# One pool of four PSUM banks, value copies for batch 0, and new costs in a planned attention and mixing kernel

## The chip, the cores and the metric

The kernel runs on one core of a Trainium2 chip. The metric is the device time of one execution in microseconds (us), as the median of several runs. The core's engines are TensorE (PE in the profile, with PEld for its weight loads), VectorE (DVE), ScalarE (ACT), GpSimd (POOL) and SyncE (SP); SP issues all DMA transfers here. TensorE writes its results into PSUM, which has eight banks of 512 fp32 words per partition.

## The reference, cut to what matters

Sizes: 8 batches, 8 heads of 64, 512 local and 32 global positions (544 rows), model width 512, hidden width 2048.

```python
# attention: a global part over all 544 keys, and a local part over a band of 65 keys and the 32 global ones
out_g = softmax(scale * q_g @ k_all.T) @ v_all
out_l = softmax([scale * q_l @ k_g.T, where(|i - j| <= 32, scale * q_l @ k_l.T, -1e9)]) @ [v_g, v_l]
x = concat(out_g, out_l) as (8, 544, 512)
# mixing and a feed-forward net
u = x + real(fft(fft(x, axis=1), axis=2))
un = (u - mean(u)) / sqrt(var(u) + 1e-6)
y = u + relu(un @ w_ch1) @ w_ch2
```

## The kernel before, in words

**Stages.** The heads of a batch are taken in four pairs p (32 pairs in all, four per batch). A pair has four units u of 128 queries. For two units together `scores` (L576) makes 24 small matmuls into the two banks of one tile S, one bank per head; `masked` (L590) on DVE adds the mask and takes the row maximum, `exps`, `p_hi` (ACT) and `p_lo` (POOL) turn that into fp16 high and low parts, `turn` (SP) transposes them by DMA into pl, and `values` (L622) multiplies with the values into a bank, from which `norm` (DVE) makes x. Two pairs form a group g, for which `g_scores`, `g_max`, `g_exp`, `g_turn`, `g_values` and `g_norm` do the same for the global queries. `x_out` stores a pair's x in DRAM. Once a batch's pairs are done, `jobs_dft` loads x back and makes the two Fourier transforms as matmuls (`d_first` L885, `d_second` L925), which gives u. The 4352 rows make 17 chunks of 256, two per batch and a last one of the 32 rows that each batch leaves over: `l_bn` to `l_turn` normalise a chunk, `f_first` (L1030) makes the hidden layer in eight steps of 24 matmuls, `f_hi` and `f_lo` evict it, and `f_second` (L1050) makes eight steps of 12 matmuls into two accumulator banks.

**Weights.** Both weight matrices come as 32 tiles of 64-bit floats. `w_load` (SP) fetches a tile into a buffer, `w_split64` (ACT) and `w_low` (POOL or ACT) take its halves, `w_size` (DVE) joins them, `w_sum` (L383, PE) sums absolute values, `w_sign` (DVE) sets the signs, `w_max` finds a scale for a group of tiles, and `w_hi` (ACT) and `w_lo` (DVE, L428) make the fp16 parts. The first `f_first` waits for the last `w_sum` (the object `wend`).

**The plan.** The order of all instructions on every engine is made on the host. `Plan.add` declares a job: engine, a cost in us, what it reads and writes, a due time t, a margin. `Plan.run` plays the jobs through with these costs: on each engine the job with the earliest due time goes next among those that are ready, and the order that results is written out (`emit`); on the chip each engine runs its list in that order, and semaphores do the waiting. A margin delays the moment from which a job counts as ready after its inputs. `rate` multiplies the declared cost of TensorE's attention jobs (`PEF` = 1.65 for pairs 0 to 3). The due times of the units of batch 0 come from `U_AT` and `U_PACE`: U_AT + U_PACE·k for unit k. Those of the weight tiles come from `W_AT`, `W2_AT` and others, and those of the chunks from `T0` and `PERIOD`. `QUEUE` limits how far ahead of the DMA work a load of q, k, v or weights is issued.

**PSUM.** The eight banks are: S (two banks, one buffer, shared by `scores` and `g_scores`), two for `ps1` (hidden layer, and weights), two accumulators (`acc0`, `acc1`), and `bk` and `bk1`, a pool of two for the outputs of `values` and of the Fourier transforms. In `bk` there are also fixed columns that the pool does not know: the result of `g_values` (columns 300 to 364) and small totals (`total` L420, `dft_scale` L764, columns from 400 on).

**Batch 0 and its values.** A unit's keys lie in two row blocks, and the second block is 96 rows: 64 local ones and 32 global ones, which lie apart in vN. For batches 1 to 7 `v_out` (L545) copies them together into vB with two DMAs per pair, and `values` makes 12 matmuls per unit (per head three of 128 rows and three of 96). For batch 0 there is no copy, and in three of a pair's four units each matmul of 96 rows is made as one of 64 and one of 32 rows.

Of the kernel before, what the change touches and what calls it, by code (L numbers as in the profile page):

```python
# [33 lines left out]
U_AT, U_PACE = 16.0, 2.0  # L34
# [8 lines left out]
PEM, SPM = 0.6, 0.2  # L43
LOOK = {"ACT": 0.5, "DVE": 0.5, "POOL": 0.8, "SP": 0.5}
ALOW = 4
L_HOLD = 50.0
QUEUE = 2.0
# [55 lines left out]
class Plan:  # L103
# [64 lines left out]
    def run(self):  # L168
# [20 lines left out]
        def ready(j):  # L189
# [5 lines left out]
            for d in j.war:  # L195
                t = max(t, d.end if d.eng == j.eng and not d.svc else d.end + self.HOP)
            for o in j.alloc:
                k = o[0]
                if k in self.pools:
                    v = [0.0 if h is None else done_at[h] if left[h] == 0 else None for h in pool[k]]  # L200
                    v = [x for x in v if x is not None]
                    if not v:
                        return None
                    t = max(t, min(v) + self.HOP)
                else:
                    h = hold[k][count[k] % len(hold[k])]
                    if h is not None:
                        if left[h]:
                            return None
                        t = max(t, done_at[h] + self.HOP)  # L210
# [6 lines left out]
        while todo:  # L217
# [28 lines left out]
            for o in j.alloc:  # L246
                k = o[0]
                if k in self.pools:
                    for i, h in enumerate(pool[k]):
                        if h is None or (left[h] == 0 and done_at[h] <= s + 1e-9):  # L250
                            pool[k][i] = o
                            self.slot[o] = i
                            break
# [20 lines left out]
class Kern:  # L274
    def __init__(self, tc, stack, ins, out):
# [49 lines left out]
        self.bk, self.bk1 = (self.ps.tile([P, 512], F32, name=f"bk{i}") for i in range(2))  # L325
# [92 lines left out]
    def total(self, a, n):  # L418
        o = 400 + 8 * n if n < 8 else 400 + 4 * n
        w = math.prod(a.shape[1:])  # L420
        pb = self.bk[:, o:o + w]
# [73 lines left out]
    def z_total(self, g):  # L495
        self.total(self.acc[g % 2], g % 8)
# [7 lines left out]
    def scales(self, g):  # L504
# [5 lines left out]
        self.scale_of(z[:, :, 3:6], g % 8)  # L510
# [64 lines left out]
    def scores(self, i):  # L575
# [3 lines left out]
        js = (2 * half, 2 * half + 1)  # L579
        s["S"] = S = self.psa.tile([P, 2, 512], F32, name="S", tag="A", bufs=1)  # L580
        for n, j in enumerate(js):
            for o in range(2):
                for m, (a, c) in enumerate(((0, 0), (0, 1), (1, 0))):
                    k0 = 512 * c + P * j
                    for h in range(2):
                        r = slice(64 * h, 64 * h + 64)
                        t = 224 * n
                        ps, k = (S[:, h, t + 192:t + 224], kg[r, c]) if o else (S[:, h, t:t + 192], kT[r, k0:k0 + 192])
                        nc.tensor.matmul(ps, qT[r, a, j], k, start=m == 0, stop=m == 2)  # L589

    def masked(self, u):
# [3 lines left out]
        S, z = s["S"], s["z"]  # L595
        for h in range(2):
            nc.vector.tensor_tensor_reduce(self.per[u % 4][:, h, 0:224], S[:, h, 224 * n:224 * n + 224], self.msk[:, j], z[:, 8:9], 3e38,  # L597
# [21 lines left out]
    def bank(self, o):  # L619
        return (self.bk, self.bk1)[self.plan.slot[o]]  # L620

    def values(self, i):  # L622
# [31 lines left out]
    def g_scores(self, g):  # L654
        nc, G = self.nc, self.G[g]
        G["sg"] = S = self.psa.tile([P, 2, 512], F32, name="S", tag="A", bufs=1)
        for m, (a, c) in enumerate(((0, 0), (0, 1), (1, 0))):
            for o in range(2):
                for i in range(2):
# [3 lines left out]
                    nc.tensor.matmul(S[64 * i:64 * i + 64, o, 0:k.shape[1]], qg, k, start=m == 0, stop=m == 2)  # L663

    def g_max(self, g):
        nc, G = self.nc, self.G[g]
        G["ng"] = ng = self.p2.tile([P, 3], F32, name="ng")
        nc.vector.tensor_reduce(ng[:, 0:1], G["sg"][:, 0], axis=EX, op=ALU.max)
        nc.vector.tensor_reduce(ng[:, 1:2], G["sg"][:, 1, 0:SG], axis=EX, op=ALU.max)
        nc.vector.tensor_scalar(ng[:, 2:3], ng[:, 0:1], ng[:, 1:2], G["z"][:, 2:3], op0=ALU.max, op1=ALU.mult)  # L670

    def g_exp(self, g):
        nc, G, pg = self.nc, self.G[g], self.pg
        sg, ng, c = G.pop("sg"), G.pop("ng"), G["z"][:, 1:2]
        nc.scalar.activation(pg[:, 32:544], sg[:, 0], AF.Exp, bias=ng[:, 2:3], scale=c)
        nc.scalar.activation(pg[:, 576:608], sg[:, 1, 0:SG], AF.Exp, bias=ng[:, 2:3], scale=c)
# [87 lines left out]
    def dft_scale(self, b):  # L764
        nc = self.nc
        pb = self.bk[:, 496 + 8 * (b % 2):501 + 8 * (b % 2)]
# [372 lines left out]
    def jobs_scores(self, add, p):  # L1139
# [16 lines left out]
        if b:  # L1156
            add("SP", 1.16, self.v_out, p, r=[vN], w=[vB], svc=1.2, t=U[0] + 7)
# [220 lines left out]
```

## Time and profile before

| | us |
|---|---|
| median of 3 runs | 1067.12 (1066.3 to 1068.29) |
| the profiled execution | 1066.91 |
| its span, first to last instruction | 1064.8 |
| TensorE busy in it | 961.5 (90%) |
| VectorE busy | 709.1 (67%) |
| ScalarE busy | 583.4 (55%) |
| GpSimd busy | 442.7 (42%) |

The span is the profiled execution without 2.1 us around it. Busy time is the union of an engine's instructions. The row DMA is the mean busy share of 16 DMA engines. A wait is idle time of an engine just before an instruction, with the instruction elsewhere that ended it. A line such as L589 is the line of the kernel before.

### The profile page before, as it was taken

To read this page: it belongs to the slowest core of one execution; us is meant where nothing else is said; L and a number is where in the kernel's file an instruction comes from. 1 tells how busy PE (TensorE), PEld (TensorE's weight loads), DVE (VectorE), ACT (ScalarE), POOL (GpSimd) and SP (SyncE) were. 2 spreads that over 40 slices of the span, in tenths; PEclk is the share of its full clock that TensorE was granted. 3 is DMA by queue.
4 is the path that set the end of the run, shared out by engine and by line. 5 is a ranking of instruction groups with operands and counts; after the bars stand their busy time and mean duration, and the time that the engine had idled before them with its cause. 6 is when DMAs were issued, how large, how long until landed. Compare 5 with 4: busy or idle time off the path is not lost.

```text
span 1064.8 us, 25495 instructions
## 1 busy us (share of the span) xinstructions
PE 961.5 (90%) x9952; PEld 671.6 (63%) x9952; DVE 709.1 (67%) x1896; ACT 583.4 (55%) x1275; POOL 442.7 (42%) x604
## 2 busy tenths in 40 slices
PE   2598358989999999999999999899999999999996
PEld 1355136656676766676777777676766666666663
DVE  6877999977888677988767897897464232431111
ACT  7976786877666766876576768754131111111110
POOL 6765546754474465566257555744010110110000
PEclk9999978989999999999999999999999999999999
DMA  9989837956785866777668757875401102111000
GB/s 365 240 197 207 283 74 144 181 149 145 140 177 128 166 144 177 147 163 182 117 139 159 195 123 160 147 145 95 115 12 54 41 20 63 23 41 40 1 21 20
DMA packets 257889, 136.81 MB, mean 128 GB/s; under 512 B 201344, under 2 KB 235744, under 8 KB 257768
## 3 DMA queue, kind: packets, MB, share of 16 engines
q1 hardware_dynamic: 257768, 135.18, 55.1%
q8 instruction: 78, 1.28, 0.5%
q14 instruction: 43, 0.35, 0.1%
HBM read 64.88 MB, written 18.35 MB: 78 GB/s over the span
## 4 chain that ended last, share of the span: by engine, by line
PE 60%; DVE 14%; issue 2%; POOL 2%; ACT 1%; DMA 1%; SPq 0%; DVEq 0%; POOLq 0%; ACTq 0%
PE ps L1039 26%; PE acc L1058 25%; PE S L589 2%; PE bk L904 1%; PE bk L934 1%; PE bk L633 1%; DVE h L1048 1%; DVE pe L597 1%; PE bk L641 1%; DMA qk<-in_qk 1%; DVE wh L428 1%; PE S L663 1%; DVE x L824 1%; POOL ph L612 1%; DVE u L959 1%
## 5 line engine op out<-in xcount | busy, mean ns | idle before, releaser
L1039 PE MATMUL ps<-uh,wh 128*128 128x256 f16 x3264 | 380.2, 274 | 0.1
L1058 PE MATMUL acc<-wh,h 128*128 128x512 f16 x1632 | 374.5, 380 | 0.0
L1039 PEld LDWEIGHTS <-wh 128*128 128x128 f16 x3264 | 317.0, 98 | 53.3 <-issue 0.8
L1058 PEld LDWEIGHTS <-h 128*128 128x128 f16 x1632 | 156.0, 98 | 168.2 <-issue 2.8
L1048 DVE SCALAR_TENSOR_TENSOR h<-ps,h 128x512 f16<-128x512 f32 x136 | 93.7, 689 | 227.8 <-ACT h L1044 227.7
L1044 ACT ACTIVATE h<-ps 128x512 f16<-128x512 f32 x136 | 80.8, 594 | 278.5 <-PE ps L1039 278.2
L612 POOL TENSOR_TENSOR ph<-pe,ph 128x448 f16<-128x448 f32 x128 | 137.4, 1086 | 171.1 <-ACT ph L608 118.2
L604 ACT ACTIVATE pe<-pe,nm 128x224 f32<-128x224 f32 x256 | 103.9, 468 | 26.1 <-DVE nm L597 26.1
L597 DVE CUSTOM_DVE_ANT_0 pe<-S,msk,z 128x224 f32<-128x224 f32 x256 | 100.8, 445 | 7.1 <-PE S L589 5.4
L1019 POOL TENSOR_TENSOR ve<-ve 128x2 f32<-128x2 f32 x17 | 4.8, 285 | 204.6 <-DVE un L999 204.6
L633 PE MATMUL bk<-vN,pl 128*128 128x65 f16 x768 | 74.2, 200 | 12.4 <-DVE xg L709 3.8
L641 PEld LDWEIGHTS <-pl 96*128 96x128 f16 (+1 forms) x840 | 63.8, 100 | 23.0 <-issue 11.1
L608 ACT ACTIVATE ph<-pe 128x448 f16<-128x448 f32 x128 | 69.1, 564 | 8.1 <-DMA pl<-ph 6.8
L589 PE MATMUL S<-kT,qT 64*128 64x192 f16 x768 | 53.7, 263 | 21.0 <-DVE nm L597 16.9
L589 PEld LDWEIGHTS <-qT 64*128 64x128 f16 x1536 | 51.0, 99 | 30.7 <-DVE nm L597 17.3
L633 PEld LDWEIGHTS <-pl 128*128 128x128 f16 x768 | 59.0, 101 | 14.0 <-issue 3.8
L543 POOL TENSOR_TENSOR vN<-vf,vN 128x640 f16<-128x640 f32 x32 | 45.2, 1412 | 16.4 <-ACT vN L539 16.3
L532 POOL TENSOR_TENSOR vf<-vf,z 128x640 f32<-128x640 f32 x32 | 41.3, 1291 | 25.5 <-DVE z L499 24.5
L1003 ACT ACTIVATE unh<-un 128x512 f16<-128x512 f32 x34 | 21.3, 628 | 47.5 <-DVE un L999 47.3
L641 PE MATMUL bk<-vN,pl 96*128 96x65 f16 (+1 forms) x336 | 46.2, 214 | 0.0
L490 ACT ACTIVATE junk<-qk 128x512 f16<-128x512 f32 x64 | 39.8, 622 | 7.7 <-DMA qk<-in_qk 6.9
L552 ACT ACTIVATE qk<-qk,z 128x512 f32<-128x512 f32 x64 | 43.2, 708 | 0.0
(179 smaller groups left out, 1398.5 us busy)
## 6 DMA issues: line engine op xcount, KB each, us to landing
qk<-in_qk SPq DMA_DIRECT2D x32, 512.0 KB
vf<-in_v SPq DMA_DIRECT2D x32, 320.0 KB
xs<-x SPq DMA_DIRECT2D x32, 256.0 KB
out<-u SPq DMA_DIRECT2D x16, 512.0 KB
rx<-in_moe_w_ch SPq DMA_DIRECT2D x14, 512.0 KB
raw<-in_moe_w_ch SPq DMA_DIRECT2D x13, 512.0 KB
x<-xs SPq DMA_DIRECT2D x48, 128.0 KB
u<-xs SPq DMA_DIRECT2D x24, 256.0 KB
```

The source lines that it names most:

```text
L543: self.nc.gpsimd.tensor_sub(vN[:, :, 1, :, 0:64], self.st[p]["vf"], vN[:, :, 0, :, 0:64])
L589: nc.tensor.matmul(ps, qT[r, a, j], k, start=m == 0, stop=m == 2)
L597: nc.vector.tensor_tensor_reduce(self.per[u % 4][:, h, 0:224], S[:, h, 224 * n:224 * n + 224], self.msk[:, j], z[:, 8:9], 3e38, op0=ALU.ad ...
L604: self.nc.scalar.activation(pe[:, h, 0:224], pe[:, h, 0:224], AF.Exp, bias=nm[:, h:h + 1], scale=-1.0)
L608: self.nc.scalar.activation(ph[:, 0, :, 0:224], self.per[i % 4][:, :, 0:224], AF.Copy)
L612: self.nc.gpsimd.tensor_sub(ph[:, 1, :, 0:224], self.per[i % 4][:, :, 0:224], ph[:, 0, :, 0:224])
L633: nc.tensor.matmul(pv[:, j % 2, h], pl[:, 4 * a + 2 * h], vN[:, j, c, h, :], start=m == 0, stop=False)
L641: nc.tensor.matmul(pv[:, j % 2, h], pl[r:e, 4 * a + 2 * h + 1], v[:, c, h, :], start=False, stop=m == 2 and e == 96)
L1039: nc.tensor.matmul(ps[:, q], wt[:, w, c0:c0 + P], uh[:, :, 4 * a + kt, :], start=n == 0, stop=n == 11)
L1044: self.nc.scalar.activation(h[:, 0], self.fps[c, fp], AF.Relu)
L1048: self.nc.vector.scalar_tensor_tensor(h[:, 1], self.fps.pop((c, fp)), 0.0, h[:, 0], op0=ALU.max, op1=ALU.subtract)
L1058: nc.tensor.matmul(self.acc_f[c][j], h[:, a, q, j * P:(j + 1) * P], self.w[1, f][:, w, :], start=f == 0 and a == 0 and w == 0, stop=f == 1 ...
```

## The change

- The tile S goes, and `bk` becomes a list of four banks, one pool of four. `scores` takes two of them (one for each head), `g_scores` two, a pair of `values` one, `g_values` one (a job of the pool now, `pvg`), and each output of the Fourier transforms one, as before. The first bank of `g_scores` is never bank 0. A job that needs n banks waits until n are free, and takes those that have been free longest. The totals stay at fixed columns of bank 0 (from 448 on), with four places for the groups' totals in the place of eight, which the plan now counts (`zt`, `dt`).
- `v_out` runs for batch 0 too, and the split into 64 and 32 rows goes.
- The margin of TensorE's attention and Fourier jobs is 1.5 us in the place of 0.6, except for pairs 0 to 5 and the transforms of batch 0. It now counts after releases of buffers too, not only after inputs. `rate` 1.65 reaches to pair 5 (`EARLY`).
- `U_AT`, `U_PACE` go from 16, 2 to 4, 4, and `QUEUE` from 2 to 4.
- Declared costs of some twenty jobs change; no instruction of theirs does.

```diff
-U_AT, U_PACE = 16.0, 2.0
+U_AT, U_PACE = 4.0, 4.0
-PEM, SPM = 0.6, 0.2
+PEM, PEM0, SPM = 1.5, 0.6, 0.2
+EARLY = 6
-QUEUE = 2.0
+QUEUE = 4.0
...
             for d in j.war:
-                t = max(t, d.end if d.eng == j.eng and not d.svc else d.end + self.HOP)
+                t = max(t, d.end if d.eng == j.eng and not d.svc else d.end + self.HOP + j.margin)
...
-                    v = [x for x in v if x is not None]
-                    if not v:
+                    v = sorted(x for x in v if x is not None)
+                    n = sum(x[0] == k for x in j.alloc)
+                    if len(v) < n:
                         return None
-                    t = max(t, min(v) + self.HOP)
+                    t = max(t, v[n - 1] + self.HOP + j.margin)
...
-        self.bk, self.bk1 = (self.ps.tile([P, 512], F32, name=f"bk{i}") for i in range(2))
+        self.bk = [self.ps.tile([P, 512], F32, name=f"bk{i}") for i in range(4)]
...
-        s["S"] = S = self.psa.tile([P, 2, 512], F32, name="S", tag="A", bufs=1)
+        s["S", half] = S = [self.bank(("bank", "S", i, h)) for h in range(2)]
...
-                if j == 3:
-                    rest = [(0, 96, vN[0:96, 4])]
-                elif b:
-                    rest = [(0, 96, vB[:, j])]
-                else:
-                    rest = [(0, 64, vN[0:64, j + 1]), (64, 96, vN[64:96, 4])]
-                for r, e, v in rest:
-                    nc.tensor.matmul(pv[:, j % 2, h], pl[r:e, 4 * a + 2 * h + 1], v[:, c, h, :], start=False, stop=m == 2 and e == 96)
+                vb = vB[:, j, c, h, :] if j < 3 else vN[0:96, 4, c, h, :]
+                nc.tensor.matmul(pv[:, j % 2, h], pl[0:96, 4 * a + 2 * h + 1], vb, start=False, stop=m == 2)
...
-        G["pv"] = pv = self.bk[:, 300:365]
+        G["pv"] = pv = self.bank(("bank", "pvg", g))[:, 0:65]
...
-        if b:
-            add("SP", 1.16, self.v_out, p, r=[vN], w=[vB], svc=1.2, t=U[0] + 7)
+        add("SP", 1.16, self.v_out, p, r=[vN], w=[vB], svc=1.2, t=U[0] + 7)
...
-        rate = PEF if p < 4 else 1.0
+        rate, pem = (PEF, PEM0) if p < EARLY else (1.0, PEM)
...
-            add("DVE", .80, self.w_lo, k, i, r=[w], w=[h], t=T + 1)
+            add("DVE", 1.15, self.w_lo, k, i, r=[w], w=[h], t=T + 1)
...
-                add("DVE", 1.80, self.d_even, b, i, r=[x4h[0]], w=[x4h[0]], k=[x4])
+                add("DVE", 2.40, self.d_even, b, i, r=[x4h[0]], w=[x4h[0]], k=[x4])
...
-        plan = self.plan = Plan(rings, {"bank": 2})
+        plan = self.plan = Plan(rings, {"bank": 4})
```

## Rows read from the trace of the kernel before

**Rows 1.** Busy time by stretch: its us, then busy us (instructions) per engine.
```profile
core 0: us, PE busy (x) PEld busy (x) DVE busy (x) ACT busy (x) POOL busy (x), PEclk, DMA share, GB/s
0.00:42.00 42.00, 11.61 (x98) 6.88 (x98) 31.25 (x79) 34.53 (x75) 29.24 (x44) 1.00 0.92 319
42.00:108.00 66.00, 57.98 (x561) 36.70 (x562) 51.52 (x140) 48.66 (x105) 38.90 (x39) 1.00 0.90 214
108.00:161.00 53.00, 22.34 (x237) 15.46 (x235) 49.41 (x135) 41.82 (x95) 28.14 (x42) 0.86 0.59 170
161.00:250.00 89.00, 79.58 (x932) 56.70 (x930) 78.95 (x191) 64.92 (x145) 53.69 (x60) 0.93 0.77 160
250.00:750.00 500.00, 484.59 (x5971) 349.73 (x5972) 400.34 (x1154) 345.88 (x776) 277.52 (x362) 1.00 0.71 149
750.00:1065.00 315.00, 305.37 (x2160) 206.09 (x2158) 97.61 (x201) 47.59 (x84) 15.22 (x60) 0.99 0.13 36
```

**Rows 2.** TensorE in order of time: start, us, what; values of two units, batch 0.
```profile
55.07 0.24 PE L633 MATMUL bk<-vN,pl 128*128 128x65 f16 x1
55.24 0.40 PE L641 MATMUL bk<-vN,pl 64*128 64x65 f16 x2
...
58.04 0.23 PE L633 MATMUL bk<-vN,pl 128*128 128x65 f16 x1
58.09 0.25 PE L641 MATMUL bk<-vN,pl 96*128 96x65 f16 x1
...
58.81 0.66 PE L589 MATMUL S<-kT,qT 64*128 64x192 f16 x6
```

**Rows 3.** Waits of DVE and of SP from 42 to 108 us: total, times, longest.
```profile
DVE wm L395 <- PE wl L391: 7.9, 5, 2.6
DVE dng L707 <- PE bk L641: 3.0, 1, 3.0
...
SPq L617 <- PE bk L641: 5.0, 4, 3.6
```

**Rows 4.** SP and TensorE in order of time: the way to the first scores.
```profile
9.59 0.33 SPq L481 DMA_DIRECT2D vf<-in_v  x1
...
16.82 0.59 PE L423 MATMUL bk<-vac,part 128*128 128x6 f32 x2 [1.39 <-ACT junk L490]
...
23.25 0.34 PE L589 MATMUL S<-kT,qT 64*128 64x192 f16 x2 [0.92 <-ACT qT L562]
```

**Rows 5.** SP and TensorE in order of time: batch 0's last store to the first hidden layer.
```profile
109.22 0.38 SPq L732 DMA_DIRECT2D xs<-x  x1
...
122.65 0.53 SPq L547 DMA_DIRECT2D vB<-vN  x1
123.51 0.74 SPq L548 DMA_DIRECT2D vB<-vN  x1
...
160.82 6.32 PE L1039 MATMUL ps<-uh,wh 128*128 128x256 f16 x48
```

**Rows 6.** TensorE in order of time: scores after a wait, and two steps of f_first.
```profile
218.42 0.66 PE L589 MATMUL S<-kT,qT 64*128 64x192 f16 x6 [4.32 <-DVE nm L597]
...
220.10 4.75 PE L1039 MATMUL ps<-uh,wh 128*128 128x256 f16 x24
...
231.06 2.78 PE L1039 MATMUL ps<-uh,wh 128*128 128x256 f16 x24
```

**Rows 7.** Waits of TensorE from 250 to 750 us: total, times, longest.
```profile
PE bk L934 <- DVE xg L709: 2.9, 2, 1.5
PE S L589 <- DVE nm L597: 2.8, 3, 1.2
PE bk L633 <- DVE xg L709: 2.0, 2, 1.3
PE bk L633 <- DVE asm L951: 1.7, 2, 1.0
...
PE S L663 <- DVE nm L597: 1.1, 1, 1.1
PE bk L633 <- DVE z L924: 1.1, 1, 1.1
...
PE bk L423 <- DVE asm L951: 0.5, 1, 0.5
```

More of the change, by code (lines that the diff above doesn't have):

```diff
@@ L248, in run @@
                 if k in self.pools:
[L249 to L253, printed above, removed]
+                    n = len(pool[k])
+                    i = min((x for x in range(o[1:2] + o[3:] == ("Sg", 0), n) if pool[k][x] is None or left[pool[k][x]] == 0),
+                            key=lambda x: (-1.0 if pool[k][x] is None else done_at[pool[k][x]], x))
+                    pool[k][i] = o
+                    self.slot[o] = i
                 else:
@@ L578, in scores @@
         qT, kT, kg = s["qT"], s["kT"], s["kg"]
-        js = (2 * half, 2 * half + 1)
-        s["S"] = S = self.psa.tile([P, 2, 512], F32, name="S", tag="A", bufs=1)
-        for n, j in enumerate(js):
+        s["S", half] = S = [self.bank(("bank", "S", i, h)) for h in range(2)]
+        for n in range(2):
+            j = 2 * half + n
+            t = 224 * n
             for o in range(2):
@@ L655, in g_scores @@
         nc, G = self.nc, self.G[g]
-        G["sg"] = S = self.psa.tile([P, 2, 512], F32, name="S", tag="A", bufs=1)
+        G["sg"] = S = [self.bank(("bank", "Sg", g, o)) for o in range(2)]
         for m, (a, c) in enumerate(((0, 0), (0, 1), (1, 0))):
@@ L1155, in jobs_scores @@
         add("POOL", 1.35, self.v_lo, p, r=[vf, vN], w=[vN], t=U[0] + 5)
-        if b:
-            add("SP", 1.16, self.v_out, p, r=[vN], w=[vB], svc=1.2, t=U[0] + 7)
+        add("SP", 1.16, self.v_out, p, r=[vN], w=[vB], svc=1.2, t=U[0] + 7)
         x = ("x", p)
         def half(h):
-            i = 2 * p + h
-            S = ("S", i)
-            add("PE", rate * .76, self.scores, i, r=[kT, qT, kg], w=[S], t=U[2 * h], margin=PEM)
+            S = [("bank", "S", 2 * p + h, o) for o in range(2)]
+            add("PE", rate * .76, self.scores, 2 * p + h, r=[kT, qT, kg], w=S, t=U[2 * h], margin=pem)
             for n in range(2):
@@ L1166, in half @@
                 pe, ph = ("pe", u), ("ph", u)
-                add("DVE", .77, self.masked, u, r=[S, z, ("msk",)], w=[pe, ("nm", u)])
+                add("DVE", .77, self.masked, u, r=[*S, z, ("msk",)], w=[pe, ("nm", u)])
                 add("ACT", .77, self.exps, u, r=[pe, ("nm", u)], w=[pe])
@@ L1177, in vals @@
                 u = 4 * p + 2 * h + n
-                add("PE", rate * .42, self.values, u, r=[("pl", u), vN] + ([vB] if b else []), w=[pv], margin=PEM)
+                add("PE", rate * .42, self.values, u, r=[("pl", u), vN, vB], w=[pv], margin=pem)
             add("DVE", .80, self.norm, i, r=[pv, z], w=[x])
@@ L1230, in jobs_dft @@
             add("ACT", .63, self.d_hi, b, i, r=[*src, dsc], w=[eh[i]], k=own)
-            add("DVE", .90, self.d_lo, b, i, r=[*src, dsc, eh[i]], w=[eh[i]], k=own)
+            add("DVE", .70, self.d_lo, b, i, r=[*src, dsc, eh[i]], w=[eh[i]], k=own)
         add("ACT", 1.48, self.d_tail_hi, b, r=[et, dsc], w=[ht])
@@ L1248, in jobs_dft @@
                 pb = self.bank_of(b, (kt, cs))
-                add("PE", rate * .54, self.d_second, b, kt, cs, r=[(f"z{cs}", b), ("const",)] + ([("zr", b)] if cs == 0 else []), w=[pb], margin=PEM, **late)
+                add("PE", rate * .54, self.d_second, b, kt, cs, r=[(f"z{cs}", b), ("const",)] + ([("zr", b)] if cs == 0 else []), w=[pb], margin=pem, **late)
                 if cs == 0:
@@ L1256, in jobs_dft @@
             for i in range(2):
-                add("DVE", 1.00, self.d_add, b, kt, i, r=[asm] + ro + o[i:i + 1], w=o[i:i + 1], **late)
+                add("DVE", 1.25, self.d_add, b, kt, i, r=[asm] + ro + o[i:i + 1], w=o[i:i + 1], **late)
         add("SP", 1.3, self.d_rest, b, r=[("xf", b), ("xm", b)], w=[("ul", b)], svc=.3)
@@ L1274, in jobs_chunk @@
             un, hl = ("un", c, j), ("unh", c, j)
-            add("DVE", .50, self.l_un, c, j, r=rj + [ve], w=[un, hl], t=L, back=LNB)
+            add("DVE", .55, self.l_un, c, j, r=rj + [ve], w=[un, hl], t=L, back=LNB)
             add("ACT", .55, self.l_hi, c, j, r=[un], w=[hl], t=L, back=LNB)
```

79 lines of the change are left out of this document (39 added, 40 removed).

## The prediction

> **What bounds the kernel now.** I read the busy time by stretch first, because the share over the whole span (TensorE 90%) hides two regimes. From 161 us on TensorE is the bound: it is busy 79.6 of 89 us, 484.6 of 500 and 305.4 of 315 [rows 1]. What is done there is fixed work, the 17 chunks of the feed-forward net and the attention of batches 1 to 7, so the end comes earlier only if TensorE starts on it earlier or idles less in it. Its idle time there is 9.4 us (161 to 250), 15.4 us (250 to 750) and some 10 us at the end, where the last outputs drain.
>
> Before 161 us no engine is the sole bound, but VectorE and the DMA engines are nearly full. VectorE is busy 49.4 of 53 us between 108 and 161, and the DMA engines 0.92 and 0.90 of the time up to 108 us [rows 1]. TensorE does 58.0 us of work in the 66 us from 42 to 108. In this stage batch 0's attention is made between the weight tiles; its last x goes out at 109.22 us, the transforms and the normalisation follow, and the first f_first begins at 160.82 us [rows 5]. So the change has two places to earn something: the date of the first f_first, and TensorE's idle time after it.
>
> I read the waits next, for what ends them, and then single jobs in order of time.
>
> **The change part by part.** All sums start from the profiled execution, 1066.9 us; it lies 0.2 us below the median of the runs, which I neglect.
>
> *A, four banks and the margin, 250 to 750 us.* The waits of TensorE here are for banks: transforms and values wait for the global norm, which reads a fixed piece of bk (2.9 and 2.0), scores and global scores wait for `masked` to leave the one buffer S (2.8 and 1.1), and values wait for a transform's result to be read (1.7 and 1.1) [rows 7]. These six make 11.6 of the 15.4 us. The global values now have a bank of their own, so 2.9 + 2.0 = 4.9 go. A second pair of banks is there for scores when no values or transforms hold it, and of the remaining 6.7 I take half, 3.3. The wider margin moves attention jobs behind a step of the feed-forward net, which is there to fill the time, so I give it 1 us more of what is left. New waits come from sharing: a job of two banks needs both free. I charge 1 us. Sum: 4.9 + 3.3 + 1 − 1 = 8 us gained; the bounds are 0 (every wait comes back in another form) and 15.4.
>
> A rule bears on what stays. A total was held up by a reader of other columns of the same bank (0.5 us, L423 after L951) [rows 7]. The Trainium skill, PSUM — Partial Sum Buffer, section PSUM bank collisions raise a hardware error, says to guard PSUM by bank, not by address, and the trace agrees. As the totals stay in bank 0, which the pool still hands out, by this rule their waits stay; the half that I took above leaves room for them.
>
> *B, the same from 161 to 250 us.* One wait of scores for `masked` is 4.32 us long. The f_first behind it took 4.75 us for 24 matmuls of 256 columns, and a later one 2.78 us [rows 6]: 0.198 us each is the 1.2 GHz level, 0.116 the 2.4 GHz one, after an idle stretch, and the granted clock of 161 to 250 us is 0.93 [rows 1]. Without the wait 4.32 + 1.97 = 6.3 us go. I keep 1.3 us back because VectorE is busy 78.95 of these 89 us and may be late at the next step. Gain 5 us, bounds 0 and 9.4 + 2.0 = 11.4.
>
> *C, the date of the first f_first.* A unit of batch 0 whose second block is split takes from 55.07 to 58.04 us, 2.97 us, and the next one, unsplit, to 58.81, at most 0.77 us [rows 2]. Three of four units are split, 12 in all, so TensorE does 12 × 2.2 = 26.4 us less. This is no gain by itself: it counts only where others wait for TensorE. From 42 to 108 us VectorE waits 7.9 us for the weight sums, which stand behind values in TensorE's order, and 3.0 us for the global values; SP waits 5.0 us for values to release pl, with weight loads queued behind [rows 3]. So VectorE's side allows up to 10.9 us. The DMA engines allow less: 0.90 × 66 = 59.4 us of work. The copies add 4 × 2 DMAs; a pair of them occupies SP 0.53 + 0.74 = 1.27 us [rows 5], 5.1 us for four, and their 146 KB each (97.5 and 48.8) at that stretch's 214 GB/s are 0.7 us, 2.7 us for four. 59.4 + 2.7 = 62.1, so if no DMA work moves out of this stretch it shrinks by 3.9 us.
>
> By one rule the split should have cost almost nothing: the Trainium skill, TensorEngine Tiling (Array Packing), Key Properties, has independent tiles work in parallel, which would make the saving 0. The same list says that a change of tiling mode drains the engine, and the trace is on that side: 0.165 us per step between pieces of different height.
>
> The new due times come on top. The group's total at 16.82 us waits for the sums of pair 1's values, whose load is issued at 9.59, behind weight loads and constants, and the first scores come at 23.25 [rows 4]. With due times 12 us earlier for the first unit this load goes ahead of the weights: 0 to 7 us. The price is that weights come later, and they too must be done before f_first, so I take 4. C is 3.9 + 4 = 8 us; bounds 17.9 (10.9 + 7) and a loss, which is a rival below.
>
> *Edits at nothing.* QUEUE lets loads be issued earlier; from 250 us on the DMA share is 0.71, so a transpose behind a longer queue has room, and the order holds attention far ahead of its chunks: all attention is over by about 750 us, with 315 us of nearly pure TensorE left [rows 1]. The same slack hides the attention's later dates under the wider margin; if it were gone, f_first would wait for its input instead. Declared costs only change the order; I give them no term, as they work through A to C.
>
> **Sum:** 8 + 5 + 8 = 21 us, 1066.9 − 21 = 1045.9, so **1046 us** (a span near 1043.8).
>
> **The rivals.**
>
> *Startup does not move (C = 0).* DMA engines and VectorE are full there [rows 1], and TensorE's shorter values become idle time. For it: 0.92 and 0.59 + VectorE 93% after 108 us. Against it: 10.9 us of VectorE's waits are for TensorE [rows 3]. 1066.9 − 13 = 1054.
>
> *The bank waits come back (A = B = 0).* Scores hold two of four banks and meet values, transforms and totals in one pool; a wait for `masked` becomes a wait for a bank. 1066.9 − 8 = 1059. Against it: two waits in rows 7 end with the global norm, which no longer shares a bank by fiat.
>
> *Everything goes better.* C at 17 (VectorE's waits and the earlier start in full), A 12, B 6: 1066.9 − 35 = 1032.
>
> *Slower.* The due times of batch 0's units stretch: the last is due at 4 + 15·4 = 64 in the place of 16 + 15·2 = 46, 18 us later against weights whose due times stay. If the order follows that, batch 0's last x goes out later than 109.22, and with it the transforms, the normalisation and the first f_first; values also wait for the copies, 5.1 us on SP. At most 18 + 5 = 23 us, less A and B: 1066.9 + 23 − 13 = 1077; with two thirds of it 1069. It turns slower once the last store comes 13 us later, at 122 us. Against it: in the trace the first scores start at 23.25 although due at 16, and the values end near 108, so the old due times were not what set the pace.
>
> **How the numbers follow.** Forecast 0.45, startup unmoved 0.15, bank waits back 0.08, better 0.15, slower 0.17. The forecast's own range is 1037 to 1052. For 8 in 10 I leave out half of the better case's tail and the outer half of the slower one: **1027 to 1071**. A difference of 0.2% (2 us) is about what a measurement of this kernel can tell from none. All of the first four cases are faster by more than that; of the slower case 0.05 falls within it, because A and B make up for part of the loss. Faster 0.82, same 0.05, slower 0.13.
>
> **What would show each step.** A: the rows "bk <- DVE xg" are gone, and TensorE's idle time from 250 to 750 us is near 7 us. B: no wait over 3 us after the first f_first. C: no L641 of 64 or 32 rows, VectorE's waits for the weight sums under 3 us, first scores near 17 to 20 us, last store of batch 0 near 101, first f_first near 153. Wrong would be a first f_first at 161 or later, or TensorE's waits for `masked` that stay as long as they were. A weak point is that the whole order is made anew: a stall at one place of the old list says only where slack is missing, not where it will be missing in the new one.

## The result and the profile after

The changed kernel took 1043.15 us (median of 4 runs, 1041.71 to 1045.34) against 1067.61 us in the same comparison: a ratio of 0.9774 (0.9753 to 0.9795), 24.5 us faster. The forecast was 1046. The profiled execution took 1045.34 us, its span is 1042.9 us, 21.9 us less than before. TensorE is busy 30 us less; VectorE, ScalarE and GpSimd are within 3 us of before. The head of the page after:

```profile
span 1042.9 us, 25368 instructions
...
PE 931.2 (89%) x9880; PEld 657.0 (63%) x9880; DVE 709.2 (68%) x1896; ACT 585.7 (56%) x1275; POOL 445.3 (43%) x604
```

Busy time by stretch of the kernel after, to be laid beside [rows 1]:

```profile
core 0: us, PE busy (x) PEld busy (x) DVE busy (x) ACT busy (x) POOL busy (x), PEclk, DMA share, GB/s
0.00:42.00 42.00, 11.67 (x111) 7.86 (x112) 27.70 (x75) 36.22 (x77) 29.07 (x43) 0.80 1.02 330
42.00:108.00 66.00, 33.59 (x474) 23.75 (x473) 58.72 (x158) 52.22 (x116) 41.71 (x46) 0.53 1.02 251
108.00:161.00 53.00, 22.32 (x378) 18.38 (x378) 50.02 (x134) 44.11 (x101) 35.32 (x33) 0.63 0.69 174
161.00:250.00 89.00, 82.78 (x933) 59.98 (x934) 73.51 (x197) 63.36 (x140) 47.15 (x66) 0.92 0.62 140
250.00:750.00 500.00, 497.45 (x5695) 353.46 (x5694) 382.66 (x1063) 327.08 (x725) 261.90 (x344) 1.00 0.65 142
750.00:1043.00 293.00, 283.38 (x2294) 193.57 (x2292) 116.59 (x272) 62.67 (x120) 30.11 (x75) 0.99 0.20 49
```

From 42 to 108 us TensorE's work fell from 58.0 to 33.6 us, mostly by the shorter values (18.1 of the 24.4 us, a_split below); from 250 to 750 us its idle time fell from 15.4 to 2.55 us. After 250 us TensorE is busy 497.45 + 283.38 = 780.8 us, before it was 484.59 + 305.37 = 790.0. By busy time, then, 9.1 us of the gain were there by 250 us, and 12.9 us are idle time that went afterwards; together 22.0.

To date the gain more closely I took the **work left** at a moment: the sum over all matmuls that start after it, each at one price for its kind (line and shape), the same for every kernel: the median distance from its start to the next start after 250 us, where the granted clock is 1.00. Start of a stage and clock then no longer blur the picture. The level of such a sum hangs on the prices (another way to take the medians puts it some 8 us lower at 200 and 250 us); the differences between kernels, which alone are used here, stay within 1 us.

| at | work left before | after | gain so far |
|---|---|---|---|
| 200 us | 821.1 | 821.4 | −0.3 |
| 250 us | 779.8 | 772.1 | 7.7 |
| 750 us | 303.9 | 280.9 | 23.0 |
| end (span) | 1064.8 | 1042.9 | 21.9 |

The start, with all the shorter values, brought nothing by 200 us; 200 to 250 us brought 8.0, and 250 to 750 us brought 15.3; after 750 us 1.1 were lost. The waits of TensorE that are left from 250 to 750 us after (total, times, longest), complete:

```profile
PE bk L425 <- ACT junk L448: 1.5, 1, 1.5
PE bk L425 <- DVE nm L599: 0.5, 2, 0.3
PE bk L763 <- ACT junk L719: 0.5, 1, 0.5
```

All belong to the small totals; the waits of scores, values and transforms of [rows 7] are gone.

The start, in order of time on SP and TensorE after: the load of pair 1's values, the group's total, the first scores, the last store of batch 0 and the first f_first, to be laid beside [rows 4, 5]:

```profile
2.13 0.91 SPq L483 DMA_DIRECT2D vf<-in_v  x2
...
10.98 0.59 PE L425 MATMUL bk<-vac,part 128*128 128x6 f32 x2 [3.18 <-ACT junk L492]
...
19.17 0.66 PE L591 MATMUL bk<-kT,qT 64*128 64x192 f16 x6
...
111.02 0.38 SPq L728 DMA_DIRECT2D xs<-x  x1
...
172.49 0.80 PE L1035 MATMUL ps<-uh,wh 128*128 128x256 f16 x3 [0.86 <-DMA uh<-unh]
```

The scores start 4.1 us earlier, and yet the last store is 1.8 us and the first f_first 11.7 us later than before. Waits of VectorE and TensorE from 42 to 108 us after:

```profile
PE wl L393 <- DVE wm L383: 12.1, 10, 3.9
...
PE bk L635 <- DMA pl<-ph: 10.0, 3, 5.3
...
DVE dng L703 <- PE bk L695: 0.9, 1, 0.9
...
DVE wm L397 <- PE wl L393: 0.2, 1, 0.2
```

VectorE hardly waits for TensorE any more (0.2 and 0.9 us; 7.9 and 3.0 in [rows 3]); TensorE waits for VectorE and for the transposes instead. One thing that then holds the start is seen between 108 and 161 us, where TensorE's longest wait is this one:

```profile
PE bk L425 <- ACT junk L448: 17.3, 1, 17.3
```

It is a total for a later batch, and it stands ahead of the first transforms of batch 0 in TensorE's order. ScalarE, in order of time: its sum for this total (L448) stands behind an eviction (L850) that waits for VectorE:

```profile
141.34 0.72 ACT L850 ACTIVATE eh<-s,dsc 128x512 f16<-128x512 f32 x1 [2.94 <-DVE s L842]
141.97 0.40 ACT L448 ACTIVATE junk<-gn 128x256 f16<-128x256 f32 x1
```

The transforms of batch 0 read the same eh, so they would wait for VectorE without the total too. VectorE prepares their input there. Three of its steps after, and the same steps before:

```profile
125.59 1.49 DVE L861 TENSOR_TENSOR st<-xt 32x255 f32<-32x255 f32 x1
...
130.79 1.63 DVE L820 TENSOR_TENSOR x<-x 128x512 f32<-128x512 f32 x1
...
134.38 1.42 DVE L832 TENSOR_TENSOR x<-x 128x258 f32<-128x258 f32 x1
```

```profile
125.64 0.41 DVE L865 TENSOR_TENSOR st<-xt 32x255 f32<-32x255 f32 x1
...
127.35 0.67 DVE L824 TENSOR_TENSOR x<-x 128x512 f32<-128x512 f32 x1
...
129.05 0.43 DVE L836 TENSOR_TENSOR x<-x 128x258 f32<-128x258 f32 x1
```

Both series start at 125.0 us; the last part of eh is written at 133.9 us before and at 142.85 us after, 9.0 us later. GpSimd in the same time: before, one idle stretch; after, one job behind the other (two of them are shown):

```profile
140.81 1.25 POOL L532 TENSOR_TENSOR vf<-vf,z 128x640 f32<-128x640 f32 x1 [15.77 <-DVE z L499]
```

```profile
126.77 2.38 POOL L614 TENSOR_TENSOR ph<-pe,ph 128x448 f16<-128x448 f32 x2
...
131.84 1.70 POOL L534 TENSOR_TENSOR vf<-vf,z 128x640 f32<-128x640 f32 x1
```

### The profile page after: what moved, and what is told of

Read it like the earlier page. It is cut to its first block, busy times and chain, and to the rows that moved or that the text cites. A ratio compares the mean times of both kernels' runs of the same rounds, so it can differ in the third digit from the quotient of the medians.

```text
span 1042.9 us, 25368 instructions
## 1 busy us (share of the span) xinstructions
PE 931.2 (89%) x9880; PEld 657.0 (63%) x9880; DVE 709.2 (68%) x1896; ACT 585.7 (56%) x1275; POOL 445.3 (43%) x604
## 4 chain that ended last, share of the span: by engine, by line
PE 78%; DVE 3%; DMA 1%; issue 1%; ACT 1%; SPq 0%; POOL 0%; ACTq 0%; POOLq 0%; DVEq 0%
PE ps L1035 33%; PE acc L1054 32%; PE bk L591 3%; PE bk L635 2%; PE bk L637 2%; PE bk L930 2%; PE bk L900 1%; PE bk L659 1%; PE bk L695 1%; PE bk L902 0%; PE bk L425 0%; DMA uh<-unh 0%; PE bk L932 0%; DMA u<-xs 0%; DVE h L1044 0%
## 5 line engine op out<-in xcount | busy, mean ns | idle before, releaser
L614 POOL TENSOR_TENSOR ph<-pe,ph 128x448 f16<-128x448 f32 x128 | 139.5, 1102 | 185.3 <-ACT ph L610 160.6
L599 DVE CUSTOM_DVE_ANT_0 pe<-bk,msk,z 128x224 f32<-128x224 f32 x256 | 100.9, 445 | 6.8 <-PE bk L591 6.1
L635 PE MATMUL bk<-vN,pl 128*128 128x65 f16 x768 | 67.1, 203 | 20.5 <-DMA pl<-ph 15.2
L610 ACT ACTIVATE ph<-pe 128x448 f16<-128x448 f32 x128 | 69.5, 566 | 10.9 <-DMA pl<-ph 8.8
L637 PEld LDWEIGHTS <-pl 96*128 96x128 f16 x768 | 58.5, 104 | 8.6 <-issue 5.2
L591 PEld LDWEIGHTS <-qT 64*128 64x128 f16 x1536 | 51.5, 99 | 19.3 <-issue 16.2
L591 PE MATMUL bk<-kT,qT 64*128 64x192 f16 x768 | 54.5, 263 | 5.8 <-DVE nm L599 3.3
L637 PE MATMUL bk<-vB,pl 96*128 96x65 f16 x576 | 51.8, 203 | 0.0
L569 POOL TENSOR_TENSOR kT<-qk,kT 128x512 f16<-128x512 f32 x32 | 40.6, 1270 | 11.3 <-ACT kT L564 9.5
```

Source lines behind the costliest of these rows:

```text
L610: self.nc.scalar.activation(ph[:, 0, :, 0:224], self.per[i % 4][:, :, 0:224], AF.Copy)
L614: self.nc.gpsimd.tensor_sub(ph[:, 1, :, 0:224], self.per[i % 4][:, :, 0:224], ph[:, 0, :, 0:224])
L637: nc.tensor.matmul(pv[:, j % 2, h], pl[0:96, 4 * a + 2 * h + 1], vb, start=False, stop=m == 2)
```

## The experiments

Twelve kernels ran. Each is judged by its median, and by the work left at 200, 250 and 750 us and the idle time of TensorE from 250 to 750 us in its trace. The trace is of one execution, which lies up to 2.2 us from the median (1045.34 against 1043.15 for the kernel after). All on one page first (idle and work left as above):

| kernel | median us | ratio to before (95%) | first f_first | left at 200 | at 250 | at 750 | idle 250–750 |
|---|---|---|---|---|---|---|---|
| before | 1067.6 | 1 | 160.8 | 821.1 | 779.8 | 303.9 | 15.4 |
| b_margin | 1059.67 | 0.9921 (0.9899–0.9944) | 164.1 | 824.4 | 776.2 | 296.4 | 9.1 |
| b_dur | 1064.67 | 0.9968 (0.9956–0.9980) | 164.4 | 820.4 | 771.5 | 301.1 | 18.3 |
| b_copy | 1070.88 | 1.0029 (1.0018–1.0041) | 159.7 | 814.9 | 773.0 | 306.8 | 22.1 |
| b_mc | 1059.81 | 0.9925 (0.9903–0.9946) | 163.0 | 820.2 | 773.6 | 295.2 | 11.6 |
| after | 1043.15 | 0.9774 (0.9753–0.9795) | 172.5 | 821.4 | 772.1 | 280.9 | 2.6 |
| a_split | 1055.11 | 0.9879 (0.9857–0.9901) | 183.5 | 833.0 | 782.9 | 290.7 | 1.2 |
| a_pool2 | 1047.08 | 0.9804 (0.9777–0.9830) | 166.6 | 815.3 | 766.4 | 281.3 | 6.6 |
| a_pem | 1052.64 | 0.9858 (0.9834–0.9882) | 170.6 | 820.6 | 771.8 | 290.8 | 9.0 |
| a_pool2_u | 1044.00 | 0.9786 (0.9759–0.9813) | 164.2 | 817.2 | 769.5 | 278.7 | 2.4 |
| a_queue | 1047.75 | 0.9811 (0.9791–0.9832) | 168.0 | 819.3 | 770.3 | 284.8 | 5.3 |
| a_t0 | 1044.83 | 0.9787 (0.9767–0.9807) | 171.9 | 822.0 | 772.6 | 281.3 | 2.3 |
| a_dur | 1059.04 | 0.9918 (0.9901–0.9934) | 180.6 | 830.4 | 783.2 | 296.7 | 5.5 |
| best_pool2 | 1048.65 | 0.9819 (0.9799–0.9840) | 158.9 | 816.9 | 769.7 | 285.9 | 7.4 |

**The values of batch 0 split again** (a_split; the kernel after, in its own order, with the copies still made).

```diff
-                vb = vB[:, j, c, h, :] if j < 3 else vN[0:96, 4, c, h, :]
-                nc.tensor.matmul(pv[:, j % 2, h], pl[0:96, 4 * a + 2 * h + 1], vb, start=False, stop=m == 2)
...
+                else:
+                    rest = [(0, 64, vN[0:64, j + 1]), (64, 96, vN[64:96, 4])]
+                for r, e, v in rest:
+                    nc.tensor.matmul(pv[:, j % 2, h], pl[r:e, 4 * a + 2 * h + 1], v[:, c, h, :], start=False, stop=m == 2 and e == 96)
```

> The changed kernel, in the same order of instructions, but with the split into 64 and 32 rows in batch 0's values again, 12 units of 2.97 us in the place of 0.77, 26.4 us more of TensorE work before 110 us (the copies are still made). Theory: the start is not set by TensorE, which idles 32 us of the 66 from 42 to 108; the time stays within 3 us of the changed kernel (1040 to 1047) and the first f_first at 172 to 176 us. Rival: the shorter values are what the gain rests on; then 1051 or more, and the first f_first 8 us or more later.

1055.11 us, 12.0 us slower than after. TensorE's busy time from 42 to 108 us, and VectorE's waits there that name TensorE:

```profile
42.00:108.00 66.00, 51.66 (x500) 32.75 (x499) 51.75 (x142) 51.08 (x113) 39.52 (x43) 1.00 0.92 245
```

```profile
DVE pe L599 <- PE bk L591: 7.8, 2, 5.0
...
DVE wm L397 <- PE wl L393: 3.4, 3, 1.6
```

TensorE's work in the stretch is 18.1 us more than after (51.66 against 33.59), VectorE waits for it again, the last store of batch 0 goes out at 123.96 and f_first comes 11 us later. The 11 us stay up to the end: 11.6 at 200 us, 9.8 at 750. The rival of the expectation came, not its theory: in the new order the start does hang on TensorE, and the shorter values are worth about 11 us of it. The 72 matmuls more would make only 4.6 us of the 18.1, at the 0.064 us a step of an unsplit unit (0.77 us for 12, [rows 2]). By the Trainium skill, TensorEngine Tiling (Array Packing), Key Properties, a change of tiling mode drains the engine; the trace agrees with 18.1 us more for the same sums.

**The pool undone** (a_pool2; S as one buffer of two banks and a pool of two, the global values in fixed columns; all else as after).

```diff
-        self.bk = [self.ps.tile([P, 512], F32, name=f"bk{i}") for i in range(4)]
+        self.bk = [self.ps.tile([P, 512], F32, name=f"bk{i}") for i in range(2)]
...
-        s["S", half] = S = [self.bank(("bank", "S", i, h)) for h in range(2)]
+        s["S"] = S = self.psa.tile([P, 2, 512], F32, name="S", tag="A", bufs=1)
...
-        G["pv"] = pv = self.bank(("bank", "pvg", g))[:, 0:65]
+        G["pv"] = pv = self.bk[0][:, 300:365]
```

> The changed kernel with only the pool undone: one tile S of two banks again, two banks for values and transforms, the global values in a fixed piece of the first; margin, copies, due times and costs as changed; the order is planned anew. Theory: the pool carries most of what TensorE no longer waits after 250 us, so its idle time from 250 to 750 us goes from 2.6 to 10 us or more and the time to 1050 to 1058. Rival: the margin and the costs do it; then the idle time stays under 5 us and the time at 1040 to 1047.

1047.08 us, 3.9 us slower than after, in the profiled executions only 0.9 us of span. The theory that the pool carries the gain falls; the rival's marks are narrowly missed too, with 6.6 us of idle time in the place of under 5. The start is even 6 us better (work left at 200 us), and 250 to 750 us gives that back:

```profile
250.00:750.00 500.00, 493.39 (x5764) 351.71 (x5764) 387.74 (x1064) 326.85 (x725) 255.38 (x342) 1.00 0.65 141
```

**The wider margin alone** (b_margin; the kernel before, with the factor 1.65 up to pair 5 that goes with it).

```diff
-PEM, SPM = 0.6, 0.2
+PEM, PEM0, SPM = 1.5, 0.6, 0.2
...
-                t = max(t, d.end if d.eng == j.eng and not d.svc else d.end + self.HOP)
+                t = max(t, d.end if d.eng == j.eng and not d.svc else d.end + self.HOP + j.margin)
```

> The kernel before with only the margin of the change: 1.5 us after inputs and releases for TensorE's attention and Fourier jobs, 0.6 for pairs 0 to 5 and the transforms of batch 0, and the factor 1.65 up to pair 5. Theory: the pool carries the gain after 250 us, the margin a third of it; TensorE's idle time from 250 to 750 us falls from 15.4 to some 10 and the time to 1060 to 1066. Rival: the margin alone removes the waits; idle time under 5 us and 1050 to 1057.

1059.67 us, 8.0 us faster than before, with two banks and the old S; 0.3 us under the range of the theory. Idle time from 250 to 750 us is 500 − 490.90 = 9.1, as the theory had it:

```profile
250.00:750.00 500.00, 490.90 (x5581) 348.95 (x5579) 370.61 (x1067) 322.40 (x719) 250.47 (x340) 0.99 0.66 140
```

**The declared costs alone** (b_dur; the kernel before, some of the twenty lines).

```diff
-            add("DVE", .80, self.w_lo, k, i, r=[w], w=[h], t=T + 1)
+            add("DVE", 1.15, self.w_lo, k, i, r=[w], w=[h], t=T + 1)
...
-                add("DVE", 1.00, self.d_add, b, kt, i, r=[asm] + ro + o[i:i + 1], w=o[i:i + 1], **late)
+                add("DVE", 1.25, self.d_add, b, kt, i, r=[asm] + ro + o[i:i + 1], w=o[i:i + 1], **late)
```

> The kernel before with only the declared costs of the change; no instruction differs, only the order. Theory: costs nearer to the traced ones help by 0 to 6 us, mostly before 250 us: 1061 to 1068. Rival: the old order failed because its costs were wrong, and with the right ones alone most of the gain is there: 1043 to 1055.

1064.67 us, 3.0 us faster, as expected. At 250 us it is 8.3 us ahead of before, and 5.5 of them are lost by 750 us, 2.9 of these in more idle time (18.3 us in the place of 15.4), nearly all waits for banks.

**The copies alone** (b_copy; the kernel before).

```diff
-        if b:
+        if True:
             add("SP", 1.16, self.v_out, p, r=[vN], w=[vB], svc=1.2, t=U[0] + 7)
```

> The kernel before with only the copies: batch 0's values use vB too, and no unit is split. Theory: the shorter values let the first f_first begin some 11 us earlier (near 150 us), as the changed kernel with the split back was 12 us slower; 1055 to 1060. Rival: the copies' eight DMAs in the full queues and what else bounds the start eat that up in this order; f_first at 158 us or later and 1063 to 1069.

1070.88 us, 3.7 us slower than before in its comparison (1067.2); f_first is as late as the rival had it, and the time is above even its 1063 to 1069. And that although the last store of batch 0 goes out at 100.8 us, 8.4 earlier. At 250 us it is 6.8 us ahead of before; at 750 us it is 2.9 behind. The busy time there and three of the waits of TensorE:

```profile
250.00:750.00 500.00, 477.86 (x5697) 339.74 (x5696) 385.87 (x1100) 330.48 (x740) 262.27 (x350) 1.00 0.64 140
```

```profile
PE bk L633 <- DVE xg L703: 3.0, 4, 1.1
...
PE bk L928 <- DVE x L646: 2.8, 1, 2.8
...
PE bk L898 <- DVE xg L703: 2.4, 2, 1.5
```

A start that is earlier by 7 us is worth less than nothing if the order behind it runs into more bank waits (22.1 us of idle time against 15.4).

**The old margin in the kernel after** (a_pem).

```diff
-PEM, PEM0, SPM = 1.5, 0.6, 0.2
+PEM, PEM0, SPM = 0.6, 0.6, 0.2
```

> The changed kernel with a margin of 0.6 us in the place of 1.5 for TensorE's attention and Fourier jobs after pair 5 (0.6 still counts after releases too). Theory: the margin carries more of the gain after 250 us than the pool; TensorE's idle time from 250 to 750 us goes from 2.6 to 8 us or more, the time to 1047 to 1053. Rival: the pool suffices; idle time under 5 us, 1041 to 1046.

1052.64 us, 9.5 us slower than after. Up to 250 us the two are equal (771.8 and 772.1 left); all of the loss lies between 250 and 750 us, as expected:

```profile
250.00:750.00 500.00, 491.03 (x5696) 348.25 (x5694) 386.05 (x1084) 330.57 (x738) 263.45 (x347) 0.99 0.66 144
```

Four banks with the narrow margin leave 9.0 us of idle time; two banks with the wide one leave 6.6 (a_pool2), and 9.1 where the old costs stand too (b_margin).

**The pool and the due times undone** (a_pool2_u; a_pool2 with this).

```diff
-U_AT, U_PACE = 4.0, 4.0
+U_AT, U_PACE = 16.0, 2.0
```

> The changed kernel with the pool undone, as in the earlier run (1047 us), and with batch 0's old due times, 16 and 2 us, as well. Theory: the new due times are what moved batch 0's end and the first f_first later and took back the 11 us that the copies gave; f_first at 155 to 162 us (166.6 with the new ones), 1037 to 1043. Rival: the due times change little of the start; f_first at 164 us or later, 1044 to 1051.

1044.00 us: the kernel after without the pool and without the new due times is as fast as the kernel after. The theory falls and the rival holds: f_first starts at 164.2 us, so the new due times are not what took back the start. TensorE's waits from 250 to 750 us, complete:

```profile
PE bk L635 <- DVE asm L947: 0.9, 1, 0.9
PE S L659 <- DVE nm L599: 0.5, 1, 0.5
PE bk L635 <- DVE xg L705: 0.3, 1, 0.3
PE bk L930 <- DVE xg L705: 0.3, 1, 0.3
PE bk L635 <- DVE ge L501: 0.3, 1, 0.3
```

These are the waits of [rows 7], for the same buffers and the same releasers, but for the global norm 0.6 us in the place of 4.9, and for `masked` to leave S 0.5 in the place of 3.9. The buffers are as scarce as before; what differs is the order, in which the margin places the jobs that want them later, behind other work.

**The short queue in the kernel after** (a_queue).

```diff
-QUEUE = 4.0
+QUEUE = 2.0
```

> The changed kernel with QUEUE at 2 us again, so that loads are issued less far ahead. Theory: little, as the DMA engines are full at the start either way; 1041 to 1047. Rival: the longer queue is what feeds the start (the first scores come at 19.2 us in the place of 23.3); 1048 to 1054, and weights and batch 0 end later.

1047.75 us, 4.6 us slower; the first scores come at 24.5 us and not at 19.2. With the long queue and the old due times they come at 23.5 (a_pool2_u), so the earlier first scores need both. That start is not the loss (1.8 us ahead at 250 us); it is lost afterwards, 3.9 behind at 750 us. The time lies between the two expectations.

**Margin and copies on the kernel before** (b_mc: the edits of b_margin and b_copy).

> The kernel before with two parts of the change alone, the margin (as in b_margin) and the copies for batch 0 (as in b_copy); one buffer S, two banks, old due times, old costs, old QUEUE. Theory: the copies put TensorE's work some 7 us ahead by 250 us, and the margin keeps that from being lost in waits after it; alone they gave -8 and +3 us, together 1044 to 1050. Rival: pool, due times and costs are needed too; then the sum of the two single runs, 1060 to 1064.

1059.81 us, as with the margin alone (1059.67); the theory (1044 to 1050) falls. The shorter values, worth 12 us in the kernel after, add nothing here. Idle time from 250 to 750 us is 500 − 488.40 = 11.6 us:

```profile
250.00:750.00 500.00, 488.40 (x5659) 346.52 (x5658) 376.44 (x1069) 326.83 (x720) 255.14 (x343) 1.00 0.66 141
```

**A control** (a_t0; the kernel after with an order changed without purpose).

```diff
-T0 = 130.0
+T0 = 130.5
```

> A control: the changed kernel with T0, from which the due times of the chunks count, at 130.5 in the place of 130.0. It is meant to do nothing; about 150 of 3251 jobs change place in the order. Both theories: within 1 us of the changed kernel if small differences between orders mean something, up to 4 us away if differences of that size (as between pool and no pool) are the accident of an order.

1044.83 us, 1.7 us from the kernel after. Differences of this size between two orders say nothing about the edit behind them; a_pool2_u (0.9) is within it, a_pool2 (3.9) and a_queue (4.6) are some two to three times as large, and so are b_dur (3.0) and b_copy (3.7). As this is one order only, it does not show how far two orders can differ by accident; of these four the sign is measured, and it may still be the accident of an order.

**Two banks with due times chosen for an early start** (best_pool2; a_pool2 with the dates of units, weights, batch 1 and chunks set anew, and with them QUEUE, L_HOLD, LOOK_BY and LN).

```diff
-W_AT, W_PACE = 7.0, 2.6
+W_AT, W_PACE = 10.91, 2.64
...
-S2_AT, S2_PACE = 190.0, 5.0
+S2_AT, S2_PACE = 166.38, 4.95
```

> A version meant to be faster: margin, copies, costs of the change, no pool of four (one buffer S, two banks), and due times chosen so that batch 0 is done earlier (weights' first due time 10.9, T0 134.15, batch 1 from 127.9, S2 166.4). Theory: with the waits after 250 us gone, what an earlier first f_first brings stays to the end; f_first at 155 to 161 us (164.2 without it) and 1034 to 1041. Rival: VectorE sets the pace up to 250 us, and the work done by then does not change; 1042 to 1047.

1048.65 us, slower than theory and rival had it. f_first starts at 158.9 us, 13.6 earlier than in the kernel after, and the work left at 250 us is 2.4 us less; idle time of 7.4 us from 250 to 750 us makes it slower all the same. No version that ran was faster than the kernel after.

**The old costs in the kernel after** (a_dur; the edits of b_dur backwards).

```diff
-                add("DVE", 1.25, self.d_add, b, kt, i, r=[asm] + ro + o[i:i + 1], w=o[i:i + 1], **late)
+                add("DVE", 1.00, self.d_add, b, kt, i, r=[asm] + ro + o[i:i + 1], w=o[i:i + 1], **late)
```

> The changed kernel with the twenty old declared costs; pool, margin, copies, due times and QUEUE as changed. Theory: the margin only works on a plan whose clock runs like the chip's; margin and copies alone gave 1060 and left 11.6 us of TensorE's idle time from 250 to 750 us, and with costs and QUEUE added, without the pool, 1044 and 2.4 us. So with the old costs the idle time comes back to 8 us or more and the time is 1051 to 1058. Rival: the pool and QUEUE make up for it; idle time under 5 us, 1042 to 1048.

1059.04 us, 15.9 us slower than after: the largest of all parts, for an edit without an instruction of its own. 9.0 us are lost by 200 us, 11.1 by 250, 15.8 by 750. The expectation got the time nearly right and the place wrong: idle time from 250 to 750 us is 5.5 us, not 8 or more, and most of the loss lies before 250 us. TensorE from 161 to 250 us, and its longest waits there:

```profile
161.00:250.00 89.00, 71.67 (x786) 51.27 (x785) 79.74 (x197) 64.84 (x146) 55.02 (x73) 0.88 0.60 144
```

```profile
PE bk L930 <- ACT asm L937: 5.3, 1, 5.3
...
PE bk L635 <- DVE asm L947: 4.2, 1, 4.2
...
PE ps L1035 <- DMA uh<-unh: 2.8, 1, 2.8
```

Transforms and values stand in an order in which they wait for ScalarE and VectorE to have read the transforms' results (L937, L947); the longest such wait in the kernel after is 0.9 us there. Most of the new costs are nearer to the times that the trace of the kernel before shows (the tail of the transform's input takes 3.05 us a job there and was declared at 2.5, now at 3.3), but not all (a step of the normalisation, `l_v`: 0.60, declared at 0.50, now at 0.80).

The pool alone on the kernel before was not run; what it is worth is known only inside the whole change.

## Why the prediction was right in the sum and wrong in its terms

**The sum.** 21 us were forecast and 24.5 came (21.6 between the profiled executions). By place: A (250 to 750 us) 15.3 in the place of 8, B (161 to 250) 8.0 in the place of 5, C (the start) −0.3 in the place of 8. Two terms were too small by 10.3 and one too large by 8.3, and 1.1 were lost after 750 us, for which there was no term. That the total came out is luck: the errors made up for each other. (B is counted from 200 us here and what came before with C. The chances of the four faster cases add up to 0.83, not 0.82.)

**A: right place, too small, and put down to the wrong part.** The marks came: the rows "bk <- DVE xg" are gone, idle time is 2.55 us (the mark was near 7). 12.9 us of the 15.3 are idle time; the other 2.4 are the same work done in less busy time. The step that failed is the split of A: 4.9 for the global values' own bank, 3.3 for the second pair of banks, 1 for the margin. The margin is worth 9.5 us (a_pem against after), all of it here, and 8.0 on the kernel before (b_margin); the pool is worth 3.9 (a_pool2), or 0.9 together with the due times (a_pool2_u), which the control does not tell from nothing; and the 4.9 come without it. I read a wait "for a buffer" as a lack of buffers. It was a job placed too close behind the one that frees the buffer, and the cure that worked was to place it later, as TensorE has other work. In this stretch the waits of totals for a reader of the same bank stayed, 0.5 us before and 0.5 after (L425 after L599). The guard by bank that the Trainium skill asks for, PSUM — Partial Sum Buffer, section PSUM bank collisions raise a hardware error, agrees with that. Ahead of the first f_first there are two more of them, and long ones, since scores and global scores may now lie in the bank of the totals (TensorE's waits from 108 to 250 us after):

```profile
PE bk L425 <- DVE nm L599: 5.4, 1, 5.4
...
PE bk L425 <- DVE ng L665: 4.2, 1, 4.2
```

Neither before nor a_pool2 has such a wait of totals for scores from 108 to 250 us. The prediction's rule named this price and looked for it only from 250 us on.

**B: right, too small.** From the first f_first to 250 us no wait of TensorE is longer than 0.9 us. From 200 to 250 us the idle time went from 5.3 to 0. The remaining 8.0 − 5.3 = 2.7 us I put down to the clock, which is argued from its row alone: 200 to 220 us before, then after (columns as in the table by stretch):

```profile
200.00:220.00 20.00, 15.69 (x223) 10.35 (x221) 19.06 (x36) 16.64 (x36) 12.47 (x12) 0.93 0.74 157
```

```profile
200.00:220.00 20.00, 20.00 (x249) 14.00 (x248) 16.27 (x51) 15.84 (x34) 11.56 (x13) 1.00 0.43 118
```

The forecast had 6.3 for both together and kept 1.3 back for VectorE, which was not late.

**C: the mechanism was right and the net was not.** Of the marks, the short matmuls, the waits of VectorE (0.2 us, under 3) and the first scores (19.17, between 17 and 20) came; the last store (111.0, not 101) and the first f_first (172.5, not 153) did not, and by the text's own words that is wrong. What was said of the shorter values holds: in the kernel after they are worth 11 us of start (a_split; the bound from VectorE's waits in the old order was 10.9). They are used up by the rest of the new order, which without them would start f_first at 183.5 us. One of its pieces is measured: the pool takes 6 us of start (a_pool2: 6.1 less left at 200 us; the control differs by 0.6 there). The two waits of totals shown above, 9.6 us, may be how; no run moves the totals alone. The due times take none of it: with two banks, the new ones leave 1.9 us less at 200 us than the old (815.3 against 817.2). Another piece is read from the two traces and no run tests it: VectorE's preparation of the transforms takes 9.0 us longer beside a busy GpSimd. It cannot be all: in a_pool2_u the nineteen operations with two inputs of that preparation take 15.9 us, nearly as long as after (16.2; before 7.7), and f_first starts at 164.2. What else holds the start stays open. The step "so I take 4" and the 3.9 were both made as if the rest of the start kept its order.

**The date of the first f_first was a poor measure.** f_first starts 11.7 us later than before, and yet the work left at 200 us is the same: TensorE did attention of the next batches first. In b_copy it starts 1.1 us earlier and 6.2 us less are left. The date names one job; where an order by hand lets other work go first, only the work left tells what a start is worth.

**Declared costs at nothing: wrong.** "I give them no term, as they work through A to C" hid the largest part: 15.9 us in the kernel after, 3.0 alone. QUEUE, at nothing too, comes to 4.6 (a_queue).

**The parts do not add up.** Undone one by one in the kernel after they cost 15.9 (costs), 12.0 (shorter values, with the copies still made), 9.5 (margin), 4.6 (QUEUE) and 3.9 (pool), together 45.9 us of a gain of 24.5. Done alone on the kernel before, margin, costs and copies gain 8.0, 3.0 and −3.7, together 7.3. What an early start wins is lost again after 250 us (b_copy, b_dur, best_pool2), unless the order behind it is free of stalls; a_pem (9.0 us of idle time) and, less so, a_dur (5.5) show that the kernel after needs the margin and the costs both for that. That a margin of 1.5 us can only absorb an error of the plan that is smaller than it, and so needs true costs, is argued: no run varied the two against each other on the same start, and a_dur, which was to show it, lost 11.1 of its 15.9 us before 250 us, where pairs 0 to 5 and the transforms of batch 0 have a margin of 0.6 in any case. How the costs bring so much there stays open.

**The rivals.** "Startup does not move" was right on its condition and 11 us off in its time, since it kept A and B at 13. From 250 us on the bank waits did not come back; in the start two did, in another form (the totals' above). The slower case did not come: the last store is 1.8 us later, not 13. "Everything goes better" had A at 12 and B at 6, nearer to what was measured than the forecast, with a C that did not come.

## What to carry to other kernels

Where a host-made order sets the engines' lists, a short stall on a buffer is first a question of the order: give the job that waits a margin, and the plan the durations that the trace shows, before more buffers are made. Measure a part by undoing it in the whole as well as by doing it alone, and run one order changed without purpose, to know how much two orders differ by chance. Judge a stage before the bound sets in by the work that is left for the bounding engine, not by the date of one job.

## What the runs showed of the hardware that was not expected

**VectorE beside GpSimd.** In the preparation of the transforms ten fp32 operations of VectorE with two inputs took 1.01 to 1.63 us after, 13.0 us in all, and 0.28 to 0.67 us before, 4.0 in all; that is the 9.0 us. GpSimd made ten operations of two inputs in that time after, and none before. All fourteen traces bear it out: of these operations of the preparation, over all batches, 1196 ran with GpSimd idle, and none took over 7% more than the shortest of its kind; 932 met a GpSimd instruction, and 604 of them took over 20% more. The Trainium skill, SBUF — State Buffer, sections Who interferes with whom and Summary: rules for kernel authors, says that a VectorE instruction with two SBUF inputs contends with a GpSimd instruction that reads SBUF, and that the second one to issue blocks until the first finishes; the traces agree with it.

**The granted clock of a stretch with little TensorE work.** From 42 to 108 us the row says 1.00 before [rows 1] and 0.53 after, yet the scores took the same time in both, and a third less later. Before from 42 to 108 us, then after from 42 to 108 us, then after from 300 to 600 us (ns: min, median, max):

```profile
L589 PE MATMUL S<-kT,qT x60: 317/364/365, 53.8 to 84.7; 64*128 64x192 f16 x60
```

```profile
L591 PE MATMUL bk<-kT,qT x60: 312/361/365, 43.0 to 88.0; 64*128 64x192 f16 x60
...
L591 PE MATMUL bk<-kT,qT x288: 238/242/254, 300.7 to 595.5; 64*128 64x192 f16 x144
```

After, the row's 0.53 is near a half, the slow level of 1.2 GHz, and before the same matmul takes as long. So the scores ran at the slow level in both kernels, and in this stretch the durations tell the clock better than the row does.
